# Seven quarter products for the last down layer of a routed feed-forward block

## The chip, the cores and the metric

One core of one Trainium2 chip runs the whole program. The metric is the time of one execution on the device, in microseconds (us). Three runs of the kernel before took 528.29, 529.92 and 529.98 us; their median is 529.92 us. A difference of about 0.3%, 1.6 us, is what a measurement of this kernel can tell from no change.

## What is computed

The program is a Nyström attention, a dense feed-forward block and a routed block of experts, one behind the other. Only the last matters here. 2,304 tokens of 512 numbers are sent each to one expert of eight, the one with the largest logit; an expert is two matrices, and a token's output is scaled by its probability:

```python
    logits = x @ w_gate
    expert_idx = np.argmax(logits, axis=1)
    ...
    h = np.maximum(np.einsum('ecd,edf->ecf', disp, w1), 0.0)
    y = np.einsum('ecf,efd->ecd', h, w2)
    ...
            out[i] = gate_w[i] * y[expert_idx[i], pos[i]]
```

With the inputs given, three units of 576 tokens each meet one expert alone, and for each of them the program computes h = max(x w1, 0), 576 x 1024, and y = h w2, 576 x 512.

## The kernel before, in words

**Precision.** Every large product is made of three products of halves: a float32 number is split into a first part `hi`, rounded to the TensorE's fp32r format, and the rest `lo`. `split` writes `hi` by a copy on ScalarE (ACT; L1052) and `lo` by a subtraction on GpSimd (POOL) or VectorE (DVE; both L1053). A product takes `hi*hi`, `hi*lo` and `lo*hi` into one bank of PSUM.

**A unit.** `run_unit(i)` computes the up layer and then the down layer of unit i (i = 0, 1, 2). The raw matrices lie in `raw1` (w1) and `raw2` (w2; these are the tiles `wi` of the first part), the split ones in `w1t`, `w1_0` and `w2s`, the split h in `hT[0]` (`hi`) and `hT[1]` (`lo`).

**Up layer of units 1 and 2.** `up_seven(m)`, m = 0 to 3, computes it by Strassen and Winograd's scheme: seven products of matrix quarters take the place of eight, and the sums that the scheme needs are made beforehand (`prepare_w`, `prepare_x`, during the down layer of the unit before; they reuse `raw1` and the tile `rx`) or from the products (`plus`, VectorE, L1140). A product is six matmuls of 288 columns (L1132) into one of six banks of the pool `ps_2`, which are taken in turn. A block m ends in four calls of `put_h`, one for each quarter of h: ScalarE writes `hT[0]` (L1079) and, for the second half of the tokens, the last 64 tokens to `h_tail` (L1081); VectorE writes `hT[1]` (L1082). `split2(f)` splits row block f of w2, f = 0 to 7, by ScalarE and GpSimd.

**Down layer.** `down_layer(t)` computes 128 rows of y, first the tail of 64 tokens (t = 4, in plain float32 from `h_tail` and `raw2`, L1170), then t = 3, 2, 1, 0: 24 matmuls of 512 columns each (8 row blocks of w2 by three products of halves, L1163) into one bank. ScalarE scales the bank by the tokens' probabilities (L1174), and a DMA stores the rows.

**The order** of this part is written by a scheduler at build time from the program's dependencies; each engine then works through its own queue in that order and waits on semaphores. So an instruction that waits holds up all that stand behind it on its engine.

Of the kernel before, what the change touches and what calls it, by code (L numbers as in the profile page):

```python
# [20 lines left out]
ON_CHIP = "made on the chip within this range"  # L21
# [104 lines left out]
def nystrom_moe_kernel(ctx, tc, qt, kt, v, w_in, w_out, w_gate, w1, w2, capacity, out, dims, dbg=None):  # L126
    nc = tc.nc
    B, H, S, D = dims
    NT, DM = out.shape
# [5 lines left out]
    P = 128  # L135
    HB = S // 2
# [3 lines left out]
    NF = QW // P  # L140
# [57 lines left out]
    prob = kp.tile([P, B, NST, 1], F32, name="prob")  # L198
# [277 lines left out]
    state, pools = {"cold": True}, {}  # L476
# [92 lines left out]
    rows = [slice(p * M, (p + 1) * M) for p in range(4)]  # L569
# [450 lines left out]
    with tc.tile_pool(name="units", bufs=1, reuse_waits="tile") as up, \  # L1020
            tc.tile_pool(name="ps_o", bufs=2, space=PSUM, reuse_waits="tile") as po, \
            tc.tile_pool(name="ps_2", bufs=6, space=PSUM, reuse_waits="tile") as p2:
        raw2 = wi
        w2s = [up.tile([P, FC, DM], F32R, name=f"w2s{a}") for a in range(2)]
        hT = [up.tile([P, FC, UNIT], F32R, name=f"hT{a}") for a in range(2)]
        h_tail = up.tile([P, FC, tail], F32, name="h_tail")
        rows_o = [up.tile([P, DM], F32, name=f"rows_o{t}") for t in range(3)]
        w1t = [[up.tile([P, KC, QW], F32R, name=f"w1s{n}{a}") for a in range(2)] for n in range(2)]
# [10 lines left out]
        mix = [[up.tile([P, HB], F32, name=f"mix{i}{k}") for k in range(4)] for i in range(2)]  # L1039
        raw1 = [up.tile([P, 2, F2], F32, name=f"raw1{i}") for i in range(2)]  # L1040
        rx = up.tile([P, NST * DM], F32, name="rx")
        rows_x = [rx[:, t * DM:(t + 1) * DM] for t in range(NST)]
        xraw = rx[:, 0:KC * S].rearrange("p (k n) -> p k n", k=KC)

        def bank(shape, name):
            t = p2.tile([P, DM], F32, tag="h", name=name)
            if len(shape) == 2:
                return t[0:shape[0], 0:shape[1]]
            return t[0:shape[0], 0:shape[1] * shape[2]].rearrange("p (a b) -> p a b", a=shape[1])

# [35 lines left out]
        def up_layer(i, f):
# [50 lines left out]
        def up_seven(m):  # L1137
# [7 lines left out]
            put_h(m, 0, y)  # L1145
            ps = product("S1", "T1", m)
            plus(w, ps, v)
            plus(u, ps, u)
            put_h(m + NF, 1, w)
            plus(v, product("A22", "T4", m), v)  # L1150
            put_h(m + NF, 0, v)
            plus(u, product("S4", "B22", m), u)
            return put_h(m, 1, u)

        def down_layer(t, gate, put):
            r = size(t)
            cols = slice(t * P, t * P + r)
            ps = po.tile([P, DM], F32, tag="o", name="ps_o")
            if r == P:
                n = 0  # L1160
                for f in range(FC):
                    for a, c in ((0, 0), (0, 1), (1, 0)):
                        nc.tensor.matmul(ps, lhsT=hT[a][:, f, cols], rhs=w2s[c][:, f, :],  # L1163
                                         start=n == 0, stop=n == 3 * FC - 1)
                        n += 1
            else:

                for n, f in enumerate(sorted(range(FC), key=lambda f: f % NF)):
                    w = n % 2
                    nc.tensor.matmul(ps[w * r:(w + 1) * r, :], lhsT=h_tail[:, f, :],  # L1170
                                     rhs=raw2[f // (FC // 2)][:, f % (FC // 2), :], start=n < 2, stop=n >= FC - 2)
            ro = rows_o[t % 3]
            if r == P:
                nc.scalar.activation(ro, ps, AF.Copy, scale=gate)  # L1174
            else:
                nc.scalar.activation(ro[0:r, :], ps[r:2 * r, :], AF.Copy)
                nc.vector.tensor_tensor(ro[0:r, :], ps[0:r, :], ro[0:r, :], op=ALU.add)
                nc.scalar.activation(ro[0:r, :], ro[0:r, :], AF.Copy, scale=gate)
            put(ro[0:r, :])

        def run_unit(i):
            more = i < B - 2
            if more and i:
                fetch(i + 1)
            for f in range(FC):
                if i == 0:
                    hi = up_layer(i, f)
                elif f < NF:
                    hi = up_seven(f)
                split2(f)  # L1190
                if i == 0 and f == 2:
                    fetch(i + 1)
            for t in range(NST):
                k = NST - 1 - t
                rows = slice(i * S + k * P, i * S + k * P + size(k))
                last = not more and t == NST - 1
                down_layer(k, prob[0:size(k), i, k, :], lambda ro: (nc.scalar if last else nc.sync).dma_start(out[rows, :], ro))
                if not more and t == NST - 3:
                    tc.mark_branch_hint_location("again", engines=(ET.SP, ET.Activation))
                    state["again"] = nc.values_load_multi_w_load_instructions(  # L1200
                        redo, min_val=0, max_val=1, skip_runtime_bounds_check_because=ON_CHIP, bass_reorder=False)[1][0]
# [158 lines left out]
        redo = up.tile([1, 1], I32, name="redo")  # L1360
        plain(redo)
        for i in range(B - 1):
            run_unit(i)
        again = state["again"]
        with ExitStack() as nest:
# [12 lines left out]
            ps = bank([P, E], "ps_n")  # L1378
# [67 lines left out]
```

## Time and profile before

| what | us |
|---|---|
| median of the three runs | 529.92 |
| the profiled execution | 529.06 |
| its span, first to last instruction | 527.3 |
| up layer of the third unit (28 products) | 474.3 to 497.0 |
| its tail (64 tokens) | 497.0 to 500.7 |
| its four blocks of 128 rows | 500.6 to 522.7 |
| last scaling, and the issue of the last store | 522.75, 523.47 |

Times inside the span are counted from its first instruction. A row of the timeline is a start, a duration, an engine, a line of the kernel, an operation, the tiles it writes and reads, its shape, and how many such stand in a row; what it waited for stands in brackets. PE is TensorE's matmul, PEld its weight loads. A matmul's end is modelled, so starts tell more than ends.

### The profile page before, as it was taken

Reading aid. Unit: us, or ns where it says so; the run is one execution under the profiler, and the core shown is the slowest. Engines: PE = TensorE matmul, PEld = TensorE weight load, DVE = VectorE, ACT = ScalarE, POOL = GpSimd, SP = SyncE. Lnnn points to the kernel's source line nnn. Section 1 sums busy time; section 2 is a strip of 40 time slices with the busy share of each in tenths; the row PEclk is TensorE's granted clock in tenths of the full one; section 3 lists DMA queues with packets and bytes.
Section 4 is the critical chain, followed back from the end, with each engine's and each line's share of the span. In section 5 each row is a group of like instructions: output and inputs, shape, how many; then the busy total and the mean of one; then the engine's idle time right before and its main releaser. Section 6 shows DMA issues by size and latency. Waiting matters only on the chain. (4 is left out here: it accounts for less than half of the span.)

```text
span 527.3 us, 12038 instructions
## 1 busy us (share of the span) xinstructions
PE 515.0 (98%) x4760; PEld 449.2 (85%) x4760; DVE 343.0 (65%) x781; ACT 293.9 (56%) x684; POOL 200.7 (38%) x254
## 2 busy tenths in 40 slices
PE   8898899999999999999999999999999999999996
PEld 6565778988889998988989999999897899689785
DVE  0789988656867876854965353357836958987700
ACT  1868878766867554744644343446346564864411
POOL 2468978987230542212513323323160070016000
PEclk9999999999999999999999999999999999999999
DMA  7896803002735521140120000129621470510011
GB/s 272 307 368 231 283 19 99 30 1 91 229 103 154 177 81 35 48 171 1 45 88 0 1 2 1 67 89 322 253 112 56 159 283 1 179 51 23 2 51 44
DMA packets 24240, 59.72 MB, mean 113 GB/s; under 512 B 2928, under 2 KB 7536, under 8 KB 24176
## 3 DMA queue, kind: packets, MB, share of 16 engines
q1 hardware_dynamic: 23360, 58.60, 31.9%
q8 instruction: 39, 0.64, 0.5%
q10 hardware_dynamic: 816, 0.28, 0.2%
q14 instruction: 25, 0.20, 0.1%
HBM read 45.89 MB, written 12.98 MB: 112 GB/s over the span
## 5 line engine op out<-in xcount | busy, mean ns | idle before, releaser
L433 PE MATMUL py<-ghi,wo 128*128 128x288 f32 x768 | 157.7, 297 | 0.0
L419 POOL TENSOR_TENSOR glo<-r,ghi 128x288 fp32r<-128x288 f32 x88 | 74.5, 849 | 137.7 <-ACT ghi L412 80.3
L433 PEld LDWEIGHTS py<-ghi,wo 128*128 128x128 f32 x768 | 123.2, 188 | 2.6 <-issue 2.0
L389 PE MATMUL ph<-at,vv 128*128 128x288 f32 x768 | 121.6, 299 | 1.0 <-DVE r L402 0.7
L389 PEld LDWEIGHTS ph<-at,vv 128*128 128x128 f32 x768 | 106.6, 188 | 11.2 <-issue 4.3
L433 PE MATMUL py<-glo,wo 128*128 128x288 f32 x384 | 113.5, 296 | 0.0
L400 ACT ACTIVATE r<-ph,half 128x288 f32<-128x288 f32 x128 | 63.5, 500 | 62.3 <-PE ph L389 33.7
L402 DVE SCALAR_TENSOR_TENSOR r<-r,ph 128x288 f32<-128x288 f32 x128 | 56.9, 450 | 48.8 <-ACT r L400 47.9
L433 PEld LDWEIGHTS py<-glo,wo 128*128 128x128 f32 x384 | 72.1, 188 | 0.0
L1163 PE MATMUL ps_o<-w2s,hT 128*128 128x512 f32 x288 | 66.2, 390 | 0.0
L1163 PEld LDWEIGHTS ps_o<-w2s,hT 128*128 128x128 f32 x288 | 53.8, 188 | 13.5 <-issue 2.4
L1053 POOL TENSOR_TENSOR w2s<-wi,w2s 128x512 fp32r<-128x512 f32 x24 | 31.6, 1344 | 87.0 <-ACT w2s L1052 87.0
L412 ACT ACTIVATE ghi<-r 128x288 fp32r<-128x288 f32 x96 | 42.1, 444 | 33.5 <-DVE r L402 33.3
L445 DVE TENSOR_TENSOR yacc<-py,yacc 128x288 f32<-128x288 f32 x72 | 32.7, 454 | 33.9 <-PE py L433 33.8
L1140 DVE TENSOR_TENSOR mix<-ps,mix 128x288 f32<-128x288 f32 x56 | 23.9, 452 | 11.6 <-PE ps L1132 10.9
L276 POOL TENSOR_TENSOR wo<-cvt,wo 128x512 fp32r<-128x512 f32 x16 | 21.0, 1313 | 24.3 <-ACT wo L274 18.9
L1079 ACT ACTIVATE hT<-mix 128x288 fp32r<-128x288 f32 x32 | 13.7, 445 | 26.8 <-DVE mix L1140 26.8
L369 DVE TENSOR_TENSOR vv<-ps_v,vv 128x512 fp32r<-128x512 f32 x32 | 21.8, 686 | 7.0 <-ACT vv L367 6.8
L735 PE MATMUL pn<-yy 128*128 128x96 f32 (+2 forms) x112 | 22.3, 293 | 2.2 <-POOL yy L687 1.5
L735 PEld LDWEIGHTS pn<-yy 128*128 128x128 f32 x112 | 17.1, 189 | 8.0 <-POOL yy L687 2.6
L1174 ACT ACTIVATE rows_o<-ps_o,prob 128x512 f32<-128x512 f32 x12 | 8.3, 689 | 24.0 <-PE ps_o L1163 19.2
L367 ACT ACTIVATE vv<-ps_v 128x512 fp32r<-128x512 f32 x32 | 18.4, 593 | 4.0 <-PE ps_v L362 3.9
(219 smaller groups left out, 831.3 us busy)
## 6 DMA issues: line engine op xcount, KB each, us to landing
raw<-in_moe_w_in SPq DMA_DIRECT2D x16, 512.0 KB, 4.0
raw<-in_moe_w_out SPq DMA_DIRECT2D x16, 512.0 KB, 4.6
wi<-in_moe_w SPq DMA_DIRECT2D x6, 1024.0 KB, 6.5
r_d<-r SPq DMA_DIRECT2D x32, 144.0 KB, 1.9
vm<-in_v SPq DMA_DIRECT2D x8, 512.0 KB, 7.2
raw<-in_moe_w SPq DMA_DIRECT2D x4, 1024.0 KB, 6.3
qT<-in_q SPq DMA_DIRECT2D x6, 576.0 KB, 6.0
qT<-in_k SPq DMA_DIRECT2D x6, 576.0 KB, 7.3
```

The source lines that it names most:

```text
L369: nc.vector.tensor_tensor(lo[:, b, :], ps[i], hi[:, b, :].bitcast(F32), op=ALU.subtract)
L389: nc.tensor.matmul(ph, lhsT=vv[pair][g][a][:, b, f * P:(f + 1) * P], rhs=at[pair][c][:, g, tok], start=n == 0, stop=n == 3 * NG - 1)
L400: nc.scalar.activation(r, ph, AF.Relu, bias=half, scale=1.0 / 6.0)
L402: nc.vector.scalar_tensor_tensor(r, r, 1.0, ph, op0=ALU.min, op1=ALU.mult)
L412: nc.scalar.activation(ghi, r, AF.Copy)
L419: nc.gpsimd.tensor_tensor(glo, r, ghi.bitcast(F32), op=ALU.subtract)
L433: nc.tensor.matmul(py, lhsT=w[a][:, f, d * P:(d + 1) * P], rhs=gh[f][c], start=f == 0 and n == 0, stop=f == NF - 1 and n == 2)
L445: nc.vector.tensor_tensor(y, py, y, op=ALU.add)
L735: nc.tensor.matmul(pn[:, cols], lhsT=yy[:, 0:P], rhs=yy[:, cols], start=True, stop=True)
L1053: engine.tensor_tensor(dst[1], src, dst[0].bitcast(F32), op=ALU.subtract)
L1140: plus = lambda dst, ps, x: nc.vector.tensor_tensor(dst, ps, x, op=ALU.add)
L1163: nc.tensor.matmul(ps, lhsT=hT[a][:, f, cols], rhs=w2s[c][:, f, :], start=n == 0, stop=n == 3 * FC - 1)
```

## The change

In the third unit (`more` is false there), the four blocks of 128 rows of the down layer are computed by the same scheme with seven products. The operands are quarters of h (256 tokens by 512 of the 1024 inner columns) and of w2 (512 by 256); each product is two blocks of 128 tokens, each twelve matmuls of 256 columns: 168 matmuls of 256 columns take the place of 96 of 512.

- `put_h(..., keep=True)` also copies h in float32 to `h32`, which lies in `raw1` (ScalarE, 16 copies, the new line L1090). The four copies of the last block m = 3 are issued in the program behind that block's other work.
- `sums_before()` stands behind `split2(3)`. GpSimd makes T1 = B12 - B11 in `rx` and T2 = B22 - T1, T1 is split into the part of `w2s` that held B12, and GpSimd makes T3 = B22 - B12 where T1 was.
- `down_seven()` follows the tail. VectorE makes S1, S3, S2, S4 and T4 (L1222) and the `lo` of seven splits, ScalarE the `hi`. The split operands lie in tiles of the up layer's weights. Ten of the fourteen blocks end in sums on VectorE (L1244), two in a copy on ScalarE, the last two in a scaling with a sum on VectorE (L1279); the rows leave by four DMAs, one of them on ScalarE's queue.

Lines from L1042 on stand one to eight lines lower in the changed file (L1053 there is L1054, L1079 is L1080, L1140 is L1148).

```diff
+        h_rows = raw2[0].rearrange("p a b -> p (a b)")[:, 0:DM]
...
-        def put_h(f, hf, x):
+        def put_h(f, hf, x, keep=False):
...
+            if keep:
+                pending.append((f, hf, x))
+                if f % NF < NF - 1 or len(pending) == 4:
+                    for f, hf, x in pending:
+                        n = min(HB, full - hf * HB)
+                        nc.scalar.activation(h32[f // NF][:, f % NF, hf * HB:hf * HB + n], x[:, 0:n], AF.Relu)
+                    pending.clear()
...
+        h32 = [t.rearrange("p a (b n) -> p (a b) n", n=full) for t in raw1]
+        early_sums = [rx[:, i * NF * P * 2:(i + 1) * NF * P * 2].rearrange("p (f n) -> p f n", f=NF) for i in range(2)]
+        places = [t[:, :, i * 2 * P:(i + 1) * 2 * P] for t in (*w1t[0], w1t[1][0], *wo[0]) for i in range(2)]
...
+        def sums_before():
+
+            (b11, b12), (b21, b22) = quarters(*raw2)
+            nc.gpsimd.tensor_tensor(early_sums[0], b12, b11, op=ALU.subtract)
+            nc.gpsimd.tensor_tensor(early_sums[1], b22, early_sums[0], op=ALU.subtract)
+            split([t[:, 0:NF, 2 * P:] for t in w2s], early_sums[0])
+            nc.gpsimd.tensor_tensor(early_sums[0], b22, b12, op=ALU.subtract)
+
+        def down_seven(i, put, flag):
...
+            where = dict(S1=a22, S2=a11, T2=t2, S3=a21, T3=t1, S4=a12, T4=b21)
+            sums = dict(S1=(a21, a22, ALU.add), S3=(a11, a21, ALU.subtract), S2=(a22, a11, ALU.subtract),
+                        S4=(a12, a11, ALU.subtract), T4=(b21, t2, ALU.subtract))
...
+            def times(a, b, m, ps):
+                n = 0
+                for f in range(NF):
+                    for x, y in ((0, 0), (0, 1), (1, 0)):
+                        nc.tensor.matmul(ps, lhsT=ops[a][x][:, f, m * P:(m + 1) * P], rhs=ops[b][y][:, f, :],
+                                         start=n == 0, stop=n == 3 * NF - 1)
+                        n += 1
+                return ps
...
+            add("S1")
+            parts_of("S1")
+            add("S3", "S2")
+            for m in pair:
+                copy(y[m], times("A11", "B11", m, new()))
+            parts_of("S2")
+            for m in pair:
+                plus(v[m], times("A12", "B21", m, new()), y[m])
+                copy(row[m][:, left], v[m], scale=gates[m])
+            parts_of("T2")
+            add("S4")
+            for m in pair:
+                plus(w[m], times("S1", "T1", m, new()), y[m])
+            parts_of("S3", "T3")
+            add("T4")
+            for m in pair:
+                ps = times("S2", "T2", m, new())
+                plus(u[m], ps, y[m])
+                plus(v[m], ps, w[m])
+            flag()
+            parts_of("S4")
+            for m in pair:
+                ps = times("S3", "T3", m, new())
...
+            parts_of("T4")
+            for m in pair:
+                plus(v[m], times("S4", "B22", m, new()), v[m])
+                copy(row[m][:, right], v[m], scale=gates[m])
+                put(m, row[m], nc.sync)
+            for m in pair:
+                nc.vector.scalar_tensor_tensor(row[m + 2][:, left], times("A22", "T4", m, new()), gates[m + 2], u[m],
+                                               op0=ALU.mult, op1=ALU.add)
+                put(m + 2, row[m + 2], nc.scalar if m else nc.sync)
...
-                    hi = up_seven(f)
+                    hi = up_seven(f, not more)
                 split2(f)
...
+                if not more and f == NF - 1:
+                    sums_before()
...
+                if not more:
+                    down_seven(i, lambda k, ro, engine, c=slice(0, DM): engine.dma_start(out[i * S + k * P:i * S + (k + 1) * P, c], ro[:, c]), flag)
+                    return
```

What the scheduler makes of this is not to be seen in the diff. Three places follow.

**GpSimd, the third unit, in the changed program** (`rx` holds T1, T2 and later T3; `wi0` and `wi1` are the two halves of the raw w2; `w2s0` its `hi`, `w2s1` its `lo`):

```order
L1201 TENSOR_TENSOR rx_5679<-wi0_121 128x1024
L1054 TENSOR_TENSOR w2s1_5657<-wi0_121,w2s0_5656 128x512 x2
L1202 TENSOR_TENSOR rx_5679<-wi1_122,rx_5679 128x1024
L1054 TENSOR_TENSOR w2s1_5657<-wi0_121,w2s0_5656 128x512 x2
L1054 TENSOR_TENSOR w2s1_5657<-wi1_122,w2s0_5656 128x512 x3
L1054 TENSOR_TENSOR w2s1_5657<-rx_5679,w2s0_5656 128x4x256
L1054 TENSOR_TENSOR w2s1_5657<-wi1_122,w2s0_5656 128x512
L1204 TENSOR_TENSOR rx_5679<-wi1_122,wi0_121 128x1024
```

Before, the eight subtractions of 128x512 stand there alone; now the first sum stands ahead of them, the second behind two of them, the `lo` of T1 and the third sum at the end.

**ScalarE, first and second block of the third unit's up layer, before** (`mix03` and `mix13` hold the first product of block 0 and of block 1, and later a quarter of h):

```order
L1141 ACTIVATE mix03_5672<-ps_7_6568 128x288
L1052 ACTIVATE w2s0_5656<-wi1_122 128x512
L1079 ACTIVATE hT0_5658<-mix03_5672 128x288
L1079 ACTIVATE hT0_5658<-mix02_5671 128x288
L1081 ACTIVATE h_tail_5660<-mix02_5671 128x64
L1079 ACTIVATE hT0_5658<-mix01_5670 128x288
L1141 ACTIVATE mix13_5676<-ps_7_6637 128x288
L1079 ACTIVATE hT0_5658<-mix00_5669 128x288
L1081 ACTIVATE h_tail_5660<-mix00_5669 128x64
L1079 ACTIVATE hT0_5658<-mix13_5676 128x288
```

**The same place in the changed program**, first its beginning:

```order
L1149 ACTIVATE mix03_5672<-ps_7_6568 128x288
L1053 ACTIVATE w2s0_5656<-rx_5679 128x4x256
L1053 ACTIVATE w2s0_5656<-wi1_122 128x512
L1080 ACTIVATE hT0_5658<-mix03_5672 128x288
L1090 ACTIVATE raw10_5677<-mix03_5672 128x288
```

and then the passage from the first block to the second:

```order
L1149 ACTIVATE mix13_5676<-ps_7_6641 128x288
L1053 ACTIVATE wo01_120<-rx_5679 128x4x256
L1053 ACTIVATE w1s10_5666<-rx_5679 128x4x256
L1080 ACTIVATE hT0_5658<-mix13_5676 128x288
L1090 ACTIVATE raw10_5677<-mix13_5676 128x288
```

The `hi` of T1 (`w2s0<-rx`) now stands ahead of the first `hT` of block 0, and the `hi` of T3 and T2 (`wo01<-rx`, `w1s10<-rx`) ahead of the first `hT` of block 1. The `hi` of T1 overwrites columns of `w2s0` that the first four subtractions on GpSimd read, and the `hi` of T3 reads the third sum.

**ScalarE, last block (m = 3) of the third unit's up layer, changed program**; before, the same rows stand there without the four copies L1090:

```order
L1149 ACTIVATE mix13_5676<-ps_7_6787 128x288
L1080 ACTIVATE hT0_5658<-mix13_5676 128x288
L1090 ACTIVATE raw10_5677<-mix13_5676 128x288
L1080 ACTIVATE hT0_5658<-mix12_5675 128x288
L1082 ACTIVATE h_tail_5660<-mix12_5675 128x64
L1090 ACTIVATE raw11_5678<-mix12_5675 128x224
L1080 ACTIVATE hT0_5658<-mix11_5674 128x288
L1090 ACTIVATE raw11_5678<-mix11_5674 128x288
L1080 ACTIVATE hT0_5658<-mix10_5673 128x288
L1082 ACTIVATE h_tail_5660<-mix10_5673 128x64
L1090 ACTIVATE raw10_5677<-mix10_5673 128x224
```

Three of the four copies stand ahead of the last `h_tail`, which the tail's last matmuls read.

## Rows read from the trace of the kernel before

**Rows 1.** The page, busy time of each engine, share of the span, instructions.

```profile
PE 515.0 (98%) x4760; PEld 449.2 (85%) x4760; DVE 343.0 (65%) x781; ACT 293.9 (56%) x684; POOL 200.7 (38%) x254
```

**Rows 2.** Busy time by stretch: start:end, length, engines with counts, granted clock, DMA, GB/s.

```profile
474.30:497.00 22.70, 22.70 (x170) 22.50 (x168) 18.02 (x40) 9.97 (x29) 9.00 (x7) 1.00 0.04 14
500.60:522.70 22.10, 22.07 (x98) 17.94 (x96) 0.68 (x1) 3.40 (x5) 0.00 (x0) 1.00 0.12 43
522.70:526.00 3.30, 0.00 (x0) 0.00 (x0) 0.00 (x0) 0.69 (x1) 0.00 (x0) 1.00 0.24 87
526.10:527.20 1.10, 0.00 (x0) 0.00 (x0) 0.00 (x0) 0.00 (x0) 0.00 (x0) 0.50 0.00 0
```

**Rows 3.** Timeline of the third unit, TensorE's products, tail and down layer, last scaling.

```profile
475.21 0.85 PEld L1132 LDWEIGHTS ps<-at,vv 128*128 128x128 f32 x6
...
482.41 0.85 PEld L1132 LDWEIGHTS ps<-w1s,w1s 128*128 128x128 f32 x6
...
497.03 3.65 PE L1170 MATMUL ps_o<-wi,h_tail 128*64 128x512 f32 x16
...
500.62 22.05 PE L1163 MATMUL ps_o<-w2s,hT 128*128 128x512 f32 x96
...
522.75 0.69 ACT L1174 ACTIVATE rows_o<-ps_o,prob 128x512 f32<-128x512 f32 x1 [4.75 <-PEq L1365]
```

**Rows 4.** Timeline of VectorE while it prepares the third unit's operands.

```profile
465.17 0.76 DVE L1125 TENSOR_TENSOR at<-rx,at 128x576 fp32r<-128x576 f32 x1
465.84 1.22 DVE L1053 TENSOR_TENSOR w1s<-raw,w1s 128x1024 fp32r<-128x1024 f32 x1
466.97 0.76 DVE L1125 TENSOR_TENSOR at<-rx,at 128x576 fp32r<-128x576 f32 x1
...
471.03 1.23 DVE L1053 TENSOR_TENSOR vv<-raw,vv 128x1024 fp32r<-128x1024 f32 x1 [0.70 <-ACT vv L1052]
472.17 0.75 DVE L1125 TENSOR_TENSOR at<-rx,at 128x576 fp32r<-128x576 f32 x1
```

**Rows 5.** Timeline: GpSimd's splits of w2 in units 1 and 2, and what runs beside.

```profile
423.26 10.32 POOL L1053 TENSOR_TENSOR w2s<-wi,w2s 128x512 fp32r<-128x512 f32 x8 [32.47 <-ACT w2s L1052]
...
471.47 3.75 ACT L1052 ACTIVATE w2s<-wi 128x512 fp32r<-128x512 f32 x7
472.17 11.13 POOL L1053 TENSOR_TENSOR w2s<-wi,w2s 128x512 fp32r<-128x512 f32 x8 [38.60 <-ACT w2s L1052]
...
478.43 0.45 ACT L1079 ACTIVATE hT<-mix 128x288 fp32r<-128x288 f32 x1 [1.82 <-DVE mix L1140]
479.11 1.55 DVE L1082 SCALAR_TENSOR_TENSOR hT<-mix,hT 128x288 fp32r<-128x288 f32 x1
480.59 0.45 DVE L1140 TENSOR_TENSOR mix<-ps,mix 128x288 f32<-128x288 f32 x1
480.96 1.18 DVE L1082 SCALAR_TENSOR_TENSOR hT<-mix,hT 128x288 fp32r<-128x288 f32 x1
```

**Rows 6.** Groups by shape, 451 to 474 us and whole run: busy, mean ns, idle before.

```profile
L1112 DVE TENSOR_TENSOR raw<-raw,raw 128x1024 f32<-128x1024 f32 x3 | 3.7, 1217 | 0.0
L1052 ACT ACTIVATE w1s<-raw 128x1024 fp32r<-128x1024 f32 x3 | 3.0, 1046 | 0.0
L687 POOL TENSOR_TENSOR yy<-yy,mask 128x128 f32<-128x128 f32 x36 | 16.9, 474 | 5.5 <-DVE yy L743 4.2 <-DVE st L662 1.1
L589 POOL TENSOR_TENSOR a<-a,mx 128x576 f32<-128x576 f32 x8 | 9.5, 1184 | 2.2 <-DVE mx L587 2.2
```

**Rows 7.** TensorE's opening matmuls: timeline row, then counts in two windows of 1.5 us.

```profile
1.55 7.64 PE L984 MATMUL warm<-ident 128*128 128x256 bf16 x43 [1.55 <-POOL ident L165]
...
5.00:6.50 1.50, 1.50 (x9) 1.07 (x8) 1.00 0.98 387
7.30:8.80 1.50, 1.50 (x15) 1.34 (x14) 1.00 1.03 405
```

More of the change, by code (lines that the diff above doesn't have):

```diff
@@ L1135, in product, with up_seven @@
             return ps
-        def up_seven(m):
+        def up_seven(m, keep=False):
             u, v, w, y = mix[m % 2]
@@ L1144, in up_seven @@
             plus(y, product("A12", "B21", m), y)
-            put_h(m, 0, y)
+            put_h(m, 0, y, keep)
             ps = product("S1", "T1", m)
@@ L1148, in up_seven @@
             plus(u, ps, u)
-            put_h(m + NF, 1, w)
+            put_h(m + NF, 1, w, keep)
             plus(v, product("A22", "T4", m), v)
-            put_h(m + NF, 0, v)
+            put_h(m + NF, 0, v, keep)
             plus(u, product("S4", "B22", m), u)
-            return put_h(m, 1, u)
+            return put_h(m, 1, u, keep)
         def down_layer(t, gate, put):
@@ L1179, in down_layer @@
             put(ro[0:r, :])
+        pending = []
+        h32 = [t.rearrange("p a (b n) -> p (a b) n", n=full) for t in raw1]
+        early_sums = [rx[:, i * NF * P * 2:(i + 1) * NF * P * 2].rearrange("p (f n) -> p f n", f=NF) for i in range(2)]
+        places = [t[:, :, i * 2 * P:(i + 1) * 2 * P] for t in (*w1t[0], w1t[1][0], *wo[0]) for i in range(2)]
+        places += [t.rearrange("p a b -> p (a b)")[:, 0:NF * 2 * P].rearrange("p (f n) -> p f n", f=NF) for t in at[0]]
+        w1d = w1t[1][1]
@@ new lines, in nystrom_moe_kernel @@
+        places += [w1d[:, :, i * 2 * P:(i + 1) * 2 * P] for i in range(2)]
+        places += [vv[0][0][a].rearrange("p a b -> p (a b)").rearrange("p (f n) -> p f n", f=NF) for a in range(2)]
+        def sums_before():
[4 more added lines that the diff above has]
+            nc.gpsimd.tensor_tensor(early_sums[0], b22, b12, op=ALU.subtract)
@@ new lines, in down_seven, with add, parts_of @@
+        def down_seven(i, put, flag):
+            (a11, a21), (a12, a22) = quarters(*h32)
+            (b11, b12), (b21, b22) = quarters(*raw2)
+            t1, t2 = early_sums
+            where = dict(S1=a22, S2=a11, T2=t2, S3=a21, T3=t1, S4=a12, T4=b21)
+            sums = dict(S1=(a21, a22, ALU.add), S3=(a11, a21, ALU.subtract), S2=(a22, a11, ALU.subtract),
+                        S4=(a12, a11, ALU.subtract), T4=(b21, t2, ALU.subtract))
+            ops = {name: places[2 * n:2 * n + 2] for n, name in enumerate(where)}
+            half_ = lambda ts, k, c: [t[:, k * NF:(k + 1) * NF, c * 2 * P:(c + 1) * 2 * P] for t in ts]
+            ops.update(T1=[t[:, 0:NF, 2 * P:] for t in w2s], A11=half_(hT, 0, 0), A12=half_(hT, 1, 0), A22=half_(hT, 1, 1),
+                       B11=half_(w2s, 0, 0), B21=half_(w2s, 1, 0), B22=half_(w2s, 1, 1))
+            def add(*names):
+                for name in names:
+                    x, y, f = sums[name]
+                    nc.vector.tensor_tensor(where[name], x, y, op=f)
+            def parts_of(*names):
+                for name in names:
+                    split(ops[name], where[name], nc.vector)
+            def times(a, b, m, ps):
[6 more added lines that the diff above has]
+                return ps
+            new = lambda: bank([P, 2 * P], "ps_d")
+            gates = [prob[:, i, t, :] for t in range(4)]
+            row = [rx[:, 2 * NF * 2 * P:2 * NF * 2 * P + DM], *rows_o]
+            row = [row[1], row[3], row[0], h_rows]
+            left, right = slice(0, 2 * P), slice(2 * P, 4 * P)
+            y, u, w, v = ([mix[m][j][:, 0:2 * P] for m in range(2)] for j in range(4))
+            copy = lambda dst, ps, **kw: nc.scalar.activation(dst, ps, AF.Copy, **kw)
+            plus = lambda dst, ps, x: nc.vector.tensor_tensor(dst, ps, x, op=ALU.add)
+            pair = range(2)
+            add("S1")
[21 more added lines that the diff above has]
+                ps = times("S3", "T3", m, new())
+                plus(w[m], ps, v[m])
+                plus(u[m], ps, u[m])
+                copy(row[m + 2][:, right], w[m], scale=gates[m + 2])
+                copy(u[m], u[m], scale=gates[m + 2])
+            parts_of("T4")
[7 more added lines that the diff above has]
+                put(m + 2, row[m + 2], nc.scalar if m else nc.sync)
@@ L1181, in run_unit, with flag @@
+        def flag():
+            tc.mark_branch_hint_location("again", engines=(ET.SP, ET.Activation))
+            state["again"] = nc.values_load_multi_w_load_instructions(
+                redo, min_val=0, max_val=1, skip_runtime_bounds_check_because=ON_CHIP, bass_reorder=False)[1][0]
         def run_unit(i):
@@ L1195, in run_unit @@
                 rows = slice(i * S + k * P, i * S + k * P + size(k))
[L1196 to L1201, printed above, removed]
+                down_layer(k, prob[0:size(k), i, k, :], lambda ro: nc.sync.dma_start(out[rows, :], ro))
+                if not more:
+                    down_seven(i, lambda k, ro, engine, c=slice(0, DM): engine.dma_start(out[i * S + k * P:i * S + (k + 1) * P, c], ro[:, c]), flag)
+                    return
                 if more and t == 0:
```

## The prediction

> **What bounds the kernel now.** I read the busy times first: TensorE has work in 98% of the span [rows 1]. The stretches confirm it for the third unit: in its up layer and in its down layer TensorE is busy throughout at the full clock, VectorE for 18.0 of 22.7 us in the one and hardly at all in the other [rows 2]. So the end is set by TensorE's queue, and the change counts by what it does to that queue: by the matmuls that it saves, and by every wait that it puts in front of one. The timeline gives the beat: nine products of the up layer go from 475.21 to 482.41, so one takes 0.80 us and one of its six matmuls 0.133 us (288 columns); 96 matmuls of 512 columns take 22.05 us, 0.230 us each; the last scaling takes 0.69 us [rows 3]. What bounds the up layer beside TensorE is the handing back of PSUM: a product's bank is free only when VectorE or ScalarE has read it, and with six banks the eleventh product needs the fifth one's.
>
> **What the change saves.** A straight line through 0.133 us at 288 columns and 0.230 us at 512 gives 0.1196 us at 256. 168 of these are 20.1 us, against 22.05: **-1.95 us**. Bounds: the opening matmuls of 256 columns (bfloat16) come 14 in 1.5 us at the faster beat, 0.107 us each [rows 7], which would give 18.0 us; 0.133 each would give 22.4. So the term lies between -4.0 and +0.4; I take the line, since both its ends are fp32r matmuls with loads of their own. At the end an operation of VectorE on 128x256 (0.45 us at 288 columns, [rows 5]; some 0.42) takes the place of 0.69 us: **-0.27 us**. The stores are as large as before.
>
> **What it adds in the down layer** is VectorE's: 5 sums and 5 `lo` of 128x1024 at 1.22 us [rows 6], 14 sums and 2 scalings at 0.42 us, the tail's addition at 0.68 us; together 19.6 us, some 18 us with the 0.08 us by which neighbours overlap, in 20.1 us. Walked in order, each operand is ready before its product: the `lo` of S2 and of S4, the tightest, by some 0.9 us. I cost it at nothing; the cover is thin, and 0.9 us more on VectorE would show on TensorE.
>
> **What it adds in the up layer.** GpSimd gets three sums and one `lo` of 128x1024. Price: 1.29 us for 128x512 (eight in 10.32 us, [rows 5]) and 0.47 us for 128x128 [rows 6] give 2.14 ns a column, so 2.4 us. Bounds: twice 1.29 is 2.6 us; 128x576 at 1.18 us, with one operand repeated [rows 6], scaled to 1024 is 2.1 us. By the Trainium skill (GPSIMD Engine Reference, Performance versus the Vector engine) an addition of 2,048 float32 columns took 4,497 ns there, so one of these would be an estimated 2.25 us, and my sum below 0.6 us smaller.
>
> GpSimd and VectorE also exclude each other. VectorE's `lo` of h, two operands from SBUF, takes 1.55 and 1.18 us while GpSimd splits w2, although its neighbour that reads PSUM takes 0.45 us; and GpSimd's eight take 11.13 us where they begin beside VectorE's, 10.32 where not [rows 5]. Each waits until the other's running instruction ends.
>
> Now the queues, in the order shown above, from the rows' own times.
> 1. T1 may start when the operand in its place has been read, at 465.93 [rows 4]. VectorE's next instruction runs until 467.06 [rows 4]; so T1 runs from 467.1 to 469.5. VectorE's `lo`, due at 466.97, waits until then; part of that goes into the idle 0.70 us at 470.3, and its last one [rows 4] ends at 474.7 in place of 472.9. Only then may GpSimd go on: two `lo` to 477.3, T2 to 479.7, the third and fourth `lo` to 482.3.
> 2. ScalarE stands at the `hi` of T1, which overwrites what these four `lo` read. It runs from 482.3 to 483.4 (1.05 us, [rows 6]), the last `hi` of w2 after it (0.54 us, seven in 3.75, [rows 5]), and the first `hi` of h ends at 484.4, where it ended at 478.9. Queued behind it on ScalarE are all of the block's `hi`; VectorE's `lo` of h waits for it, then until 484.9 for GpSimd's running `lo`, and behind that stands the addition that frees the fifth bank: 485.7. TensorE is due at the eleventh product at 482.41 and gets it at 485.8: **3.4 us idle**.
> 3. VectorE's next three `lo` of h stand behind one GpSimd instruction each (1.29, 2.4 and 1.29 us). TensorE's twelfth, fourteenth and fifteenth product wait for the additions behind them: 0.8, 0.4 and 1.6, together **2.8 us**.
> 4. GpSimd ends T3 at about 493.5. ScalarE waits for it at the `hi` of T3, ahead of the second block's `hi` of h; with the `hi` of T2 (1.05 us each) the latter ends at 496.0. TensorE's nineteenth product waits **2.1 us**.
> 5. From there the backlog is ScalarE's and VectorE's: 16 more copies of about 0.4 us, and two `lo` of 1.22 us in the last block. The last `h_tail` comes at 510.2; TensorE has reached the tail at 505.3 and done three of four pairs of its matmuls by 508.3, and waits **2.6 us** with the restart. I count the copies where the order shows them, ahead of that `h_tail`.
>
> Together 10.9 us of waits. **Sum: 10.9 - 1.95 - 0.27 = +8.7 us**, made against the profiled execution's 529.06 us: 537.8 us. That execution lies 0.86 us under the median of the runs; between 537.8 and 538.6 I forecast **538.2 us**.
>
> **The rivals.**
> *The clock falls (0.10).* Ahead of 522.7 TensorE worked without a pause, after it not at all, and the granted clock was still full until 526.0 and half after 526.1 [rows 2]: a pause of some 3.4 us ended at 1.2 GHz, and my first wait is as long. The Trainium skill (TensorE: Matmul & The Clock Gate, HAM oscillation) says that pauses of TensorE throttle it again and the next stretch begins cold. At the start the matmuls came 7 in 1.5 us first and 14 in 1.5 us later [rows 7], and the slow beat lasted from 1.55 us to beyond 6.5. Some 5 us at half speed cost up to 2.5 us where TensorE sets the pace, nothing where it waits anyway; twice that if it falls again at the tail: 538 to 543, say 541 us. Against it: the wait is just at the length seen.
> *GpSimd and VectorE don't exclude each other on these long sums (0.14).* Then only the true dependencies are left: ScalarE behind the fourth `lo` (3.2 us) and the backlog at the tail (2.6): 529.06 + 5.8 - 2.2 = 532.7 us. Against it: the two long `lo` of [rows 5].
> *Faster (0.09): GpSimd is in time.* It decides at GpSimd's fourth `lo`: done at 478.9 or sooner, 3.4 us earlier than I have it, it costs TensorE nothing. For it: GpSimd is idle for 38.6 us before 472.17 [rows 5], and raw w2 lies there well before. That needs T1 and T2 at 0.7 us each in place of 2.4, or both before 472; T2 can't be, since it waits for VectorE's last `lo` at 472.9. If the later sums hide as well, the saving is left: 529.06 - 2.2 = 526.8 us.
> *About the same (0.03)*: the first wait shrinks to some 2 us, and the later ones vanish.
> *That the change doesn't do what it says*: one part doesn't. The copies are said to go behind the tail, and the order has three of the last four ahead of the last `h_tail`. This is in step 5; it is no case of its own.
>
> **How the numbers follow.** Forecast case 0.64, clock 0.10, no exclusion 0.14, faster 0.09, same 0.03. The price of the sums (2.1 to 2.6 us) moves the forecast by about 4 us for each us, -1.2 to +0.8; the matmul's bounds move it by -2.0 to +2.3. The range of 532 to 543 us takes in the forecast with these, the no-exclusion case and nearly all of the clock's; outside lie the 0.12 of faster and same, and a rest. By more than 0.3% faster: 0.09; within it 0.03; slower 0.88.
>
> **What would show it.** Right: GpSimd's row runs from 467 to about 494 almost without a pause; ScalarE idles before the `hi` of T1 until about 482 and before that of T3 until about 493, both times ended by GpSimd; `lo` of h of 1.2 to 2.9 us; TensorE pauses of 3.4 us at 482 and some 2 us at 495 and before the tail's end, waiting for VectorE or ScalarE; the tail ends at about 511 in place of 500.7, and the fourteen blocks take 20.1 us without a pause. Wrong: an up layer that ends by 498, a down layer above 21 us, a granted clock under 1.00 in these stretches, or a 128x1024 sum on GpSimd far from 2.4 us.

## The result: 536.32 us, 1.47% slower

Four runs of the changed kernel took 536.03 to 539.83 us, median 536.32; four of the kernel before, on the same chip, 528.29 to 529.98, median 529.85. The ratio is 1.0147, its 95% interval 1.0125 to 1.0168: slower by 6.6 to 8.9 us, 7.8 by the ratio itself (the two medians lie 6.5 us apart). The forecast was 538.2 us, the range 532 to 543.

The profiled execution took 536.15 us, its span 534.4 us against 527.3. Its busy times, in answer to [rows 1]:

```profile
PE 515.9 (97%) x4832; PEld 452.7 (85%) x4832; DVE 365.3 (68%) x809; ACT 307.3 (58%) x714; POOL 210.9 (39%) x258
```

TensorE's busy share fell by only one point. The stretches show where it stood still, against 100% in [rows 2] (start:end, length, then PE, PEld, DVE, ACT, POOL, each with its count, granted clock, DMA share, GB/s):

```profile
474.30:497.00 22.70, 18.63 (x122) 17.54 (x122) 11.93 (x22) 13.16 (x33) 17.59 (x11) 0.92 0.04 14
...
482.50:484.50 2.00, 0.00 (x0) 0.00 (x0) 1.13 (x3) 1.93 (x6) 2.00 (x3) 1.00 0.00 0
485.50:488.50 3.00, 2.97 (x13) 2.62 (x12) 2.85 (x5) 1.83 (x6) 3.00 (x2) 0.50 0.01 3
```

In the up layer's stretch TensorE works 18.63 us of 22.70; from 485.5 to 488.5 it has half the clock. The timeline of TensorE's products tells each pause, in answer to [rows 3]; its last row is VectorE's last operation, which ends the program's work:

```profile
474.34 0.96 PE L1140 MATMUL ps<-xw,w1s 128*128 128x288 f32 x6
...
481.54 0.96 PE L1140 MATMUL ps<-at,wo 128*128 128x288 f32 x6
484.61 1.42 PE L1140 MATMUL ps<-w1s,w1s 128*128 128x288 f32 x6 [2.11 <-DVE mix L1148]
486.06 1.81 PE L1140 MATMUL ps<-at,wo 128*128 128x288 f32 x6
...
490.06 1.05 PE L1140 MATMUL ps<-xw,w1s 128*128 128x288 f32 x6 [0.26 <-DVE mix L1148]
...
495.18 1.06 PE L1140 MATMUL ps<-at,wo 128*128 128x288 f32 x6 [1.67 <-DVE mix L1148]
...
503.41 2.79 PE L1178 MATMUL ps_o<-wi,h_tail 128*64 128x512 f32 x12
508.07 1.08 PE L1178 MATMUL ps_o<-wi,h_tail 128*64 128x512 f32 x4 [1.86 <-ACT h_tail L1082]
509.08 6.02 PE L1232 MATMUL ps_d<-w2s,hT 128*128 128x256 f32 x48
514.94 3.04 PE L1232 MATMUL ps_d<-w2s,w1s 128*128 128x256 f32 x24
517.82 3.04 PE L1232 MATMUL ps_d<-w1s,w1s 128*128 128x256 f32 x24
...
529.60 0.48 DVE L1279 SCALAR_TENSOR_TENSOR wi<-ps_d,prob,mix 128x256 f32<-128x256 f32 x1 [0.94 <-PE ps_d L1232]
```

Here 474.34 is the third unit's first product, 481.54 the tenth and 484.61 the eleventh, 490.06 the fifteenth, 495.18 the nineteenth, 503.41 the tail's first twelve matmuls and 508.07 its last four. VectorE ended the pauses of the up layer, ScalarE that of the tail. What stood behind them, on GpSimd, ScalarE and VectorE, in answer to [rows 4, 5]:

```profile
465.80 3.31 POOL L1201 TENSOR_TENSOR rx<-wi 128x1024 f32<-128x1024 f32 x1 [32.41 <-DVE at L1133]
473.64 2.90 POOL L1054 TENSOR_TENSOR w2s<-wi,w2s 128x512 fp32r<-128x512 f32 x2 [4.53 <-ACT w2s L1053]
476.50 2.39 POOL L1202 TENSOR_TENSOR rx<-wi,rx 128x1024 f32<-128x1024 f32 x1
478.86 6.46 POOL L1054 TENSOR_TENSOR w2s<-wi,w2s 128x512 fp32r<-128x512 f32 x5
485.28 2.58 POOL L1054 TENSOR_TENSOR w2s<-rx,w2s 128x1024 fp32r<-128x1024 f32 x1
...
489.28 2.61 POOL L1204 TENSOR_TENSOR rx<-wi,wi 128x1024 f32<-128x1024 f32 x1
...
481.43 1.06 ACT L1053 ACTIVATE w2s<-rx 128x1024 fp32r<-128x1024 f32 x1 [3.87 <-POOL w2s L1054]
482.39 0.61 ACT L1053 ACTIVATE w2s<-wi 128x512 fp32r<-128x512 f32 x1
482.91 0.43 ACT L1080 ACTIVATE hT<-mix 128x288 fp32r<-128x288 f32 x1
...
491.93 1.06 ACT L1053 ACTIVATE wo<-rx 128x1024 fp32r<-128x1024 f32 x1 [4.06 <-POOL rx L1204]
...
466.77 2.95 DVE L1133 TENSOR_TENSOR at<-rx,at 128x576 fp32r<-128x576 f32 x1
...
483.37 0.82 DVE L1083 SCALAR_TENSOR_TENSOR hT<-mix,hT 128x288 fp32r<-128x288 f32 x1 [4.03 <-ACT hT L1080]
484.11 0.45 DVE L1148 TENSOR_TENSOR mix<-ps,mix 128x288 f32<-128x288 f32 x1
```

ScalarE waits 3.87 us for GpSimd's fourth difference, copies T1, ends the last `hi` of w2, and only then begins the first `hi` of h, at 482.91; VectorE's `lo` of it and the addition at 484.11 follow, and TensorE's eleventh product. At 491.93 ScalarE has waited 4.06 us for the third sum.

The account of the whole goes by starts. The third unit's first product began at 474.34 now; before, it was this row:

```profile
474.55 0.96 PE L1132 MATMUL ps<-xw,w1s 128*128 128x288 f32 x6
```

| part | before, us | after, us | difference |
|---|---|---|---|
| start of the third unit | 474.55 | 474.34 | -0.21 |
| up layer, to the tail's first matmul | 22.48 | 29.07 | +6.59 |
| tail | 3.59 | 5.67 | +2.08 |
| blocks, to the start of the last operation | 22.13 | 20.52 | -1.61 |
| last operation | 0.69 | 0.48 | -0.21 |
| from its end to the span's end | 3.86 | 4.32 | +0.46 |
| span | 527.3 | 534.4 | +7.1 |

### The profile page after: what moved, and what is told of

Read it like the earlier page. It is cut to its first block, busy times and chain, and to the rows that moved or that the text cites. A ratio compares the mean times of both kernels' runs of the same rounds, so it can differ in the third digit from the quotient of the medians.

```text
span 534.4 us, 12257 instructions
## 1 busy us (share of the span) xinstructions
PE 515.9 (97%) x4832; PEld 452.7 (85%) x4832; DVE 365.3 (68%) x809; ACT 307.3 (58%) x714; POOL 210.9 (39%) x258
## 4 chain that ended last, share of the span: by engine, by line
PE 83%; DVE 7%; ACT 4%; POOL 3%; issue 2%; DMA 0%; ACTq 0%; DVEq 0%; POOLq 0%
PE py L433 27%; PE ph L389 17%; PE ps_o L1171 8%; PE ps_h L1102 5%; PE ps L1140 4%; PE ps_d L1232 4%; PE ps_v L362 3%; PE pn L735 3%; POOL w2s L1054 2%; PE ps_o L1178 2%; PE warm L984 1%; PE ps_w L299 1%; PE ps_f L537 1%; PE pw L715 1%; PE pb L578 1%
## 5 line engine op out<-in xcount | busy, mean ns | idle before, releaser
L1054 POOL TENSOR_TENSOR w2s<-wi,w2s 128x512 fp32r<-128x512 f32 x24 | 31.3, 1331 | 53.0 <-ACT w2s L1053 53.0
L1171 PE MATMUL ps_o<-w2s,hT 128*128 128x512 f32 x192 | 44.1, 390 | 0.0
L1171 PEld LDWEIGHTS ps_o<-w2s,hT 128*128 128x128 f32 x192 | 35.9, 188 | 9.0 <-issue 1.6
L1148 DVE TENSOR_TENSOR mix<-ps,mix 128x288 f32<-128x288 f32 x56 | 23.5, 451 | 10.7 <-PE ps L1140 6.3
L1083 DVE SCALAR_TENSOR_TENSOR hT<-mix,hT 128x288 fp32r<-128x288 f32 x32 | 19.2, 608 | 9.3 <-ACT hT L1080 7.9
L1080 ACT ACTIVATE hT<-mix 128x288 fp32r<-128x288 f32 x32 | 13.8, 438 | 19.9 <-DVE mix L1148 19.9
```

## Experiments

Times are set beside the kernel before of the same chip, whose medians were 528.80, 528.88 and 529.12 us in the three groups of runs.

**The sums alone.** Theory: GpSimd and VectorE exclude each other; rival: only dependencies count.

```diff
 # the kernel before, behind split2(3) of the third unit; nobody reads s
...
+nc.gpsimd.tensor_tensor(s[0], b12, b11, op=ALU.subtract)
+nc.gpsimd.tensor_tensor(s[1], b22, s[0], op=ALU.subtract)
+nc.gpsimd.tensor_tensor(s[0], b22, b12, op=ALU.subtract)
```

> The kernel before with GpSimd's three sums of w2 added in the third unit, whose results nobody reads; the down layer, ScalarE's queue and all else stay. Theory (GpSimd and VectorE exclude each other): though nothing waits for a result, VectorE's differences of h stand behind GpSimd's sums and the PSUM banks come back late; TensorE pauses in the up layer, longest about 2 us near 488, together 2 to 4.3 us: 532 to 534 us. Rival (no exclusion, only dependencies count): nobody waits for the sums, the up layer runs without a pause: 529.9 us, within 0.6.

532.03 us, ratio 1.0054 (1.0035 to 1.0072): 1.9 to 3.8 us slower. The timeline of GpSimd, VectorE and TensorE:

```profile
465.32 3.31 POOL L1196 TENSOR_TENSOR rx<-wi 128x1024 f32<-128x1024 f32 x1 [32.41 <-DVE at L1125]
...
465.16 1.22 DVE L1053 TENSOR_TENSOR w1s<-raw,w1s 128x1024 fp32r<-128x1024 f32 x1
466.30 2.95 DVE L1125 TENSOR_TENSOR at<-rx,at 128x576 fp32r<-128x576 f32 x1
...
482.33 3.16 DVE L1082 SCALAR_TENSOR_TENSOR hT<-mix,hT 128x288 fp32r<-128x288 f32 x2
...
500.46 0.83 DVE L1082 SCALAR_TENSOR_TENSOR hT<-mix,hT 128x288 fp32r<-128x288 f32 x2
...
485.92 1.06 PE L1132 MATMUL ps<-xw,w1s 128*128 128x288 f32 x6 [0.70 <-DVE mix L1140]
```

The first sum is issued while VectorE's 1.22 us operation still runs, and shows 3.31 us; the second sum, issued between GpSimd's own, shows 2.42. VectorE's next, 0.76 us in [rows 4], shows 2.95 us and ends 0.6 us after the sum: each waited for the other. Two `lo` of h take 3.16 us at 482.33 where two take 0.83 at 500.46. The rival falls. The pauses were set too long: the up layer took 24.40 us against 22.48 (1.9 us more), and the longest pause was 0.7 us. The profiled execution, at 530.36 us, was the fastest of the five, so its rows account for some 1.9 us of the 2.9 that the ratio gives.

By the Trainium skill (SBUF — State Buffer, Who interferes with whom) an operation of VectorE with two inputs from SBUF and one of GpSimd that reads SBUF contend for a port that is locked, not shared: whichever issues first holds it for its whole instruction. The rows above agree: 2.95 and 3.31 us on one side and the other.

**Without the copied quarter's wait.** B12 is not read by the seven products, only overwritten by T1's parts.

```diff
-split2(f)
+split2(f, DM if more or f >= NF else 2 * P)   # columns 0:n only
```

> The changed kernel, but the quarter B12 of w2, which the seven products never read, is not split in the third unit: ScalarE and GpSimd split 256 instead of 512 columns of the first four row blocks, and the first part of T1 no longer overwrites what GpSimd still reads. Theory (ScalarE's wait behind GpSimd's fourth difference makes the first pause): the first part of T1 is written by 476, the first pause of TensorE falls from 2.1 to at most 1.1 us, the later ones stay in part: 531 to 533.5 us. Rival (the sums' time on GpSimd and the exclusion alone set the pauses): 535 to 536.5 us.

532.41 us, ratio 1.0062 (1.0040 to 1.0084), by the ratio 3.3 us over the kernel before, where the change had 7.8. The `hi` of T1 was written at 475.45, and of the pauses these were left (475.62 is the third unit's first product, 500.45 the tail's first matmul):

```profile
475.62 0.96 PE L1140 MATMUL ps<-xw,w1s 128*128 128x288 f32 x6
...
485.02 1.06 PE L1140 MATMUL ps<-at,wo 128*128 128x288 f32 x6 [0.41 <-DVE mix L1148]
...
489.06 1.07 PE L1140 MATMUL ps<-xw,w1s 128*128 128x288 f32 x6 [1.10 <-DVE mix L1148]
...
500.45 2.79 PE L1178 MATMUL ps_o<-wi,h_tail 128*64 128x512 f32 x12
504.58 1.08 PE L1178 MATMUL ps_o<-wi,h_tail 128*64 128x512 f32 x4 [1.33 <-ACT h_tail L1082]
```

The eleventh product, which waited 2.1 us in the change, comes on time; the first pause left is 0.41 us ahead of the twelfth, and the one of 1.67 us at the nineteenth is gone. ScalarE's wait made the first pause, as step 2 had it. GpSimd also had less to do here (its first four differences took 3.39 us; in the change 2.90 for two alone), so the run does not part the wait from the work by itself. But T2, the `lo` of T1 and T3, 7.4 us of GpSimd's work, still lie in its up layer, which took 24.83 us: 2.35 more than before, where the change lost 6.59.

**Filling the pause.** Did the fall of the clock cost 1.8 us of its own?

```diff
...
+for _ in range(14):   # between the tenth and the eleventh product
+    last = nc.tensor.matmul(idle[:, 0:HB], lhsT=wq["A11"][0][:, 0, 0:P], rhs=xq["B11"][0][:, 0, :], start=True, stop=True)
```

> The changed kernel with 14 matmuls of 288 columns more, into a bank nobody reads, between the tenth and the eleventh product of the third unit, where TensorE pauses 2.1 us; they take 1.87 us of it. Theory (behind the slow clock stood the next waits for VectorE, which come anyway): the granted clock stays 1.00 from 482 to 490, but the fifteenth product still begins near 490 and the time stays 536.3 us, within 0.6. Rival (the fall of the clock cost its own 1.8 us): 534.5 us.

536.64 us, ratio 1.0146 (1.0123 to 1.0168), as the change. Stretch and timeline:

```profile
481.00:490.00 9.00, 7.32 (x50) 6.38 (x48) 6.47 (x8) 4.84 (x13) 9.00 (x7) 1.00 0.01 2
...
484.66 1.05 PE L1140 MATMUL ps<-w1s,w1s 128*128 128x288 f32 x6 [0.31 <-DVE mix L1148]
...
490.13 1.06 PE L1140 MATMUL ps<-xw,w1s 128*128 128x288 f32 x6 [1.09 <-DVE mix L1148]
```

The clock stays full, and yet the fifteenth product begins at 490.13 (490.06 in the change). What the slow matmuls had taken is now pauses of 0.40 and 1.09 us, among others: the bank came back no sooner. Here the fall of the clock cost nothing.

**ScalarE's copies behind h.** All work stays; the `hi` of T1, T2 and T3 go behind the last operation on h.

```diff
-split([t[:, 0:NF, 2 * P:] for t in w2s], early_sums[0])
+with tc.issue_after(state["hi"]):   # and likewise round the splits of T2 and T3
+    split([t[:, 0:NF, 2 * P:] for t in w2s], early_sums[0])
```

> The changed kernel with ScalarE's three first parts of T1, T2 and T3 behind its last operation on h; the amount of work is the same. Theory (ScalarE's queue, standing at these copies, makes the two large pauses of the up layer): what is left there are pauses of 0.3 to 0.7 us from the exclusion, together under 2.5 us, and the tail begins by 500 in place of 503.4; the later parts of T1, T2 and T3 then come late for the down layer, which pauses some 4 us more: 533 to 536.5 us in all. Rival (GpSimd's work on VectorE's path makes the pauses, wherever ScalarE's copies stand): the tail begins at 502.5 or later, and the time is 537 us or more.

534.30 us, ratio 1.0103 (1.0080 to 1.0126), inside the theory's 533 to 536.5. The tail began at 497.42 and no product of the up layer began more than 0.11 us late, with one of GpSimd's sums, T2, in it (T1 runs ahead of the up layer, as in the change); the parts of T1 then came late:

```profile
497.42 2.79 PE L1178 MATMUL ps_o<-wi,h_tail 128*64 128x512 f32 x12
...
502.21 2.51 POOL L1054 TENSOR_TENSOR w2s<-rx,w2s 128x1024 fp32r<-128x1024 f32 x1 [14.72 <-ACT w2s L1053]
504.80 3.27 POOL L1205 TENSOR_TENSOR rx<-wi,wi 128x1024 f32<-128x1024 f32 x1
...
502.48 3.32 DVE L1223 TENSOR_TENSOR raw<-raw 128x1024 f32<-128x1024 f32 x1
505.72 3.43 DVE L1054 TENSOR_TENSOR w1s<-rx,w1s 128x1024 fp32r<-128x1024 f32 x1
...
510.94 2.89 PE L1237 MATMUL ps_d<-w2s,w1s 128*128 128x256 f32 x22 [2.71 <-DVE w1s L1054]
```

So ScalarE's place in the chain is what the large pauses of the up layer need. This order moves the `lo` of T1 and the third sum out of the up layer too; but two runs had such work in it and no copy on ScalarE that waited for it: the sums alone (T2 and T3) lost 1.9 us there, and the run without the copied quarter's wait (T2, T3 and the `lo` of T1) 2.35, against 6.59 in the change. In the down layer the exclusion costs again: VectorE's operations of 1.22 us take 3.32 and 3.43 beside GpSimd's. The blocks took 25.3 us, against 20.52.

**Thin copies.** Each of the 16 float32 copies of h cut to one column.

```diff
...
-                        nc.scalar.activation(h32[f // NF][:, f % NF, hf * HB:hf * HB + n], x[:, 0:n], AF.Relu)
+                        nc.scalar.activation(h32[f // NF][:, f % NF, hf * HB:hf * HB + 1], x[:, 0:1], AF.Relu)
```

> The changed kernel with each of the 16 float32 copies of h cut to one column (so that S1 to S4 come out of other numbers; order and dependencies stay). Theory (step 5 of the prediction: the copies ahead of the last h_tail are a part of the backlog that TensorE meets in the tail): 16 times some 0.3 us leave ScalarE's queue, the pause in the tail falls from 1.9 us to about 0.7 and the time by 0.8 to 1.6 us, to 6.2 to 7.0 us over the kernel before. Rival (ScalarE's copies fit into its idle time, and VectorE's two long differences of T3 and T2 make the backlog): the pause stays above 1.5 us, the time within 0.5 us of the changed kernel's.

535.70 us, ratio 1.0141 (1.0124 to 1.0159): 6.6 to 8.4 us over the kernel before. The pause in the tail fell as the theory said, from 1.86 to 0.60 us:

```profile
495.15 1.07 PE L1139 MATMUL ps<-at,wo 128*128 128x288 f32 x6 [2.07 <-DVE mix L1147]
...
506.74 1.08 PE L1177 MATMUL ps_o<-wi,h_tail 128*64 128x512 f32 x4 [0.60 <-ACT h_tail L1082]
```

The time did not follow. The up layer took 29.46 us in place of 29.07 (two `lo` of h now stood ahead of the addition for the nineteenth product, a pause of 2.07 us), and from the last operation's end to the span's end it took 5.2 us in place of 4.3. The copies are 1.3 us of the tail's pause; as a gain in time this is a miss.

**A version with VectorE's sums.** What VectorE has to do in the up layer was cut, and the sums put between its other operations.

```diff
...
+            used = not (keep and hf and f < NF)
...
+                if m == 0:
+                    nc.vector.tensor_tensor(early_sums[0], b12, b11, op=ALU.subtract)
...
+                    split([t[:, 0:NF, 2 * P:] for t in w2s], early_sums[0], nc.vector)
+                    nc.vector.tensor_tensor(early_sums[1], b22, early_sums[0], op=ALU.subtract)
+                if m == 1:
+                    nc.vector.tensor_tensor(early_sums[0], b22, b12, op=ALU.subtract)
...
+                put(m + 2, row[m + 2], nc.sync, right)
...
```

> A version meant to keep the saving. (1) B12 is not split. (2) The quarter of h that only sums read (first 512 inner columns, second half of the tokens) gets no hi and lo of its own. (3) VectorE makes T1, its lo and T2 behind the first block's h and T3 behind the second's; GpSimd is left with eight differences, four of them half as wide. (4) The splits of T2 and T3 and the last block's copies stand behind the last h_tail. (5) The last two row blocks are stored in halves, the first half early. Theory: VectorE's operations of 1.22 us fit between its others as the six banks allow; pauses in the up layer under 1 us together, none in the tail, under 0.6 us in the down layer, which keeps its 20.2 us; the last store lands in 2 us in place of 2.5: 1 to 2 us under the kernel before. Rival (VectorE is full in the up layer, and what is taken from GpSimd comes back there as waits): 0.5 to 2 us over the kernel before.

529.21 us, ratio 0.9995 (0.9979 to 1.0012). VectorE's T1, T2 and `lo` of T1, and TensorE's tail, down layer and the end:

```profile
481.80 1.22 DVE L1209 TENSOR_TENSOR rx<-wi 128x1024 f32<-128x1024 f32 x1
...
483.30 1.22 DVE L1212 TENSOR_TENSOR rx<-wi,rx 128x1024 f32<-128x1024 f32 x1
484.44 1.22 DVE L1054 TENSOR_TENSOR w2s<-rx,w2s 128x1024 fp32r<-128x1024 f32 x1
...
496.66 3.65 PE L1184 MATMUL ps_o<-wi,h_tail 128*64 128x512 f32 x16
500.25 6.01 PE L1251 MATMUL ps_d<-w2s,hT 128*128 128x256 f32 x48
...
520.99 0.48 DVE L1299 SCALAR_TENSOR_TENSOR wi<-ps_d,prob,mix 128x256 f32<-128x256 f32 x1 [0.83 <-PE ps_d L1251]
521.50 0.37 ACTq L1328 DMA_DIRECT2D out<-wi  x1
```

Up layer 22.60 us, tail 3.59, blocks 20.74: the theory's terms for TensorE held, and the last operation ended at 521.47, some 1.5 us sooner than before by the unit's own clock (47.4 us from its first product, against 48.9). But from there to the span's end (526.5) it took 5.0 us in place of 3.86, and the last store landed in 2.8 us, not in 2. Neither the theory's time nor the rival's came out.

**The same with GpSimd's two early sums.**

```diff
...
-                    nc.vector.tensor_tensor(early_sums[0], b12, b11, op=ALU.subtract)
...
-                    nc.vector.tensor_tensor(early_sums[1], b22, early_sums[0], op=ALU.subtract)
...
+            nc.gpsimd.tensor_tensor(early_sums[0], b12, b11, op=ALU.subtract)
+            nc.gpsimd.tensor_tensor(early_sums[1], b22, early_sums[0], op=ALU.subtract)
...
+                if not more and f == 0:
+                    sums_before()
```

> The version before this one, but with T1 and T2 by GpSimd, T1 as early as its place allows and T2 between the differences of w2; VectorE keeps T1's lo (behind the first block) and T3 (behind the second). Theory (each GpSimd instruction holds up VectorE's next operation with two operands from SBUF, by up to 2.4 us): pauses of 1 to 2.4 us more in the up layer than with VectorE alone, 0.3 to 1.5 us over the kernel before. Rival (as with ScalarE's copies behind, GpSimd's two early sums cost TensorE nothing): as fast as the version before this one or faster, 1 to 2 us under the kernel before.

530.60 us, ratio 1.0027 (1.0014 to 1.0040): by the ratio 1.4 us over the kernel before, inside the theory's 0.3 to 1.5. The up layer took 23.51 us, 0.9 more than with VectorE alone, just under the theory's 1 to 2.4.

**The stores in halves**, in that version and in the change, with the change itself beside them.

```diff
...
+put(m, row[m], nc.sync, left)     # behind the second product
...
+put(m + 2, row[m + 2], nc.sync, right)    # behind the fifth; the version had this line already
...
-put(m, row[m], nc.sync)
+put(m, row[m], nc.sync, right)    # behind the sixth
...
```

> The version with VectorE's sums, and all four row blocks stored in halves, each as soon as it is there: two halves after the second product, two after the fifth, and only 128 KB each for the four that are left behind the sixth and the seventh. Theory (the saving of the down layer was there, and the rows stored together at the end gave it back): from the end of the last operation to the end of the span 3.7 to 4.1 us in place of 5.0, 0.8 to 2 us under the kernel before. Rival (the number of transfers at the end counts, not their bytes: still four within 3 us): 4.7 us or more, the time as the kernel before's, within 0.5.

> The changed kernel, with its four row blocks stored in halves in the same way and nothing else. Theory (of its time some 0.5 us is the bunched stores): from the last operation's end to the span's end 3.7 to 4.0 us in place of 4.3, and 0.3 to 0.7 us less than the changed kernel beside it. Rival (number of transfers): 4.3 us or more, no gain.

> The changed kernel itself, on the chip of this group, to set the others beside: 6.5 to 8.9 us over the kernel before (by the interval of its first comparison), the pause of 2.1 us before the eleventh product and a granted clock of one half after it.

The version: 528.07 us, ratio 0.9986 (0.9974 to 0.9998); some 0.7 us under the kernel before, the only one whose interval lies under it, and by less than the 0.3% that a measurement tells with ease. The change: 538.55 us, 1.0183 (1.0166 to 1.0199), by the medians 9.4 us over the kernel before and so outside the 6.5 to 8.9 that was expected; the pause of 2.1 us and the half clock behind it came as expected. With halves: 536.20 us, 1.0130 (1.0115 to 1.0145). Both with halves came out lower, the change by 2.3 us where 0.3 to 0.7 was expected. Not all of that need be the stores': two of the four executions of the change had a mean granted clock of 0.987 and 0.988 and took 539.41 and 539.61 us, the other two 0.993 and 0.995 and 537.7 and 537.5 us, and all four with halves had 0.995. Nor do the profiled executions show the end as the reason. From the end of the last operation to the span's end the version took 4.6 us (521.81 to 526.4; the theory had 3.7 to 4.1, the rival 4.7 or more), the change with halves 5.9 (529.94 to 535.8) and the change itself 5.2 (530.62 to 535.8), where its first profile had 4.3. One kernel's end varies by 0.9 us between two executions, so one profile does not decide on half a microsecond there. How much the stores cost stays open.

## Why the prediction held

Its sign, its range and its mechanism were right: ScalarE's copies behind GpSimd's sums hold up the banks in the up layer, and more is lost there than the seven products save. Each wait came out smaller than its term. By its steps:

- **The saving on TensorE.** Taken at 0.1196 us a matmul; 24 go from 514.94 to 517.82, 0.120 each, 20.16 us for 168. The blocks took 20.52 us, so 1.61 us were saved and not 1.95: the rest is the start of the first block and the way to the last operation. The ending saved 0.21 for 0.27.
- **VectorE in the down layer** cost nothing, as put; no pause stands among the 168 matmuls.
- **The price of a sum on GpSimd**, 2.4 us: T2 took 2.39, the `lo` of T1 2.58, T3 2.61 beside VectorE. By the Trainium skill's page (GPSIMD Engine Reference, Performance versus the Vector engine) it was an estimated 2.25 us; T2's row lies nearer to ours.
- **Step 2, the first wait**, was sized 3.4 us and came to 2.27 (due at 482.34, begun at 484.61). The chain was the one described; its start was early: GpSimd's differences waited only for ScalarE's `hi` and began at 473.64 in place of 474.7, and the fourth ended at 481.43 in place of 482.3.
- **Step 3**, 2.8 us for the next products: the fifteenth was due four products of 0.80 us behind 484.61, at 487.81, and began at 490.06, 2.25 us late. In this execution part of it was a slow clock, which the filled pause showed to cost nothing: there, at the full clock, the fifteenth began 2.27 us late.
- **Step 4**, 2.1 us: 1.83 (due at 493.35, begun at 495.18). **Step 5**, 2.6 us: 2.08, of which the thin copies took 1.3.
- **The stores, "as large as before"**, were put at nothing. This is the one step with no term where there was one: the rows now leave by four stores within some 4 us, and from the last operation to the span's end it took 4.32 us in place of 3.86. That the stores lie so close may be the cause; the runs with halves did not show it.
- **Its signs.** A granted clock under 1.00 was named as a sign of being wrong, and the up layer's stretch has 0.92; the filled pause took that away and the time stayed, so the sign misled. GpSimd's row was to run almost without a pause, and had one of 4.53 us, as step 1's own times imply.
- **The rivals.** The clock did fall, behind a pause of 2.1 us, shorter than the length of 3.4 on which the rival rested, and cost nothing. Its price came from the slower beat of the opening matmuls, but both stretches of [rows 7] show a granted clock of 1.00, so those rows do not show a slow clock. That long sums exclude nothing is refuted by the sums alone. GpSimd was not in time: its fourth difference ended 2.5 us after the 478.9 that would have done.

Waits of 10.9 us were forecast. By these rows they are 2.27, 2.25, 1.83 and 2.08 us, 8.4 together, 2.5 less. The saving, the ending and the stores came out 0.9 us worse than forecast in all, so the errors partly cancel; that the profiled execution lies only 1.6 us under the sum is in part luck.

## What to carry to other kernels

Work given to an idle engine is not hidden because that engine is idle: look at who stands in a queue behind its result. Here the sums alone cost 2.9 us, and with copies on ScalarE that wait for them ahead of h the whole change lost 7.8; with one of the waits taken away, by not splitting a quarter that is only overwritten, 3.3 us were left. The 1.6 us saved on TensorE hardly showed in any version's time: with the sums on an engine that had room for them (VectorE, between its other operations) the up layer's waits were gone, and by the ratio some 0.7 us was left of it at best. So the end of the program is to be read as a term of its own.

## What was not expected of the hardware

The granted clock fell to one half behind a pause of 2.1 us in three profiles of this form (the change twice, and with its stores in halves), and not after pauses of 2.11 and 2.07 us with thin copies, nor after one of 2.71 us with ScalarE's copies behind h (the row at 510.94: 22 matmuls in 2.89 us). The length of a pause alone does not decide. Far ahead of the change, at some 56 us, TensorE pauses for 1.5 us in all twelve profiles; behind it the clock fell to one half until about 60 us in two of them (without the copied quarter's wait, and GpSimd's two early sums) and in no other. There the fall cost time: from one group of matmuls, at 53 us, to the next of the same line these two took 20.28 and 20.30 us, the kernel before 18.80. So one kernel's executions can differ by some 1.5 us for a reason that lies outside the change.

Also, the time from the last operation to the span's end was 3.86 us before and 3.8 with the sums alone, and between 4.3 and 5.9 us in the ten profiles whose down layer ends with seven products; what sets it within these bounds was not found.
